# A one-core mLSTM and two MLPs: first MLP in five passes, 512 columns a product in three, stacked scores, a new order

## Chip, core and metric

The kernel runs on one core of a Trainium2 chip. The metric is device time in microseconds (us) of one execution; the profiled execution has a span inside it, from the first to the last instruction.

## What is computed

Three stages follow each other. `S`=768, `H`=8 heads, `D`=40, two batches; 1536 tokens reach the MLPs.

```python
def _attn_ref(q, k, v, i_gate, f_gate, o_gate):          # per batch and head, step t:
    m_new = maximum(f[t] + m, i[t])
    C = exp(f[t] + m - m_new) * C + exp(i[t] - m_new) * outer(v[t], k[t])
    n = exp(f[t] + m - m_new) * n + exp(i[t] - m_new) * k[t]
    y[t] = sigmoid(o_gate[t]) * (C @ q[t]) / maximum(abs(n @ q[t]), 1.0)

x = y as (1536, 320)
x = ((x @ w_a) * (x @ w_b)) @ w_out                      # first MLP, 1536 hidden
h = x @ w_in;  out = (h * sigmoid(h)) @ w_out2           # second MLP, 2048 hidden
```

## The kernel before

**Units.** The tokens are cut into twelve units of 128 (`u` = chunk * 2 + batch; chunk `c` of six). The recurrence is done by chunk: scores of a unit (`scores`, part `uN.s0`/`.s1`, four heads each), weighed with the decays (`weigh`), summed with the values (`values`), plus what the state of the chunk before gives (`carried`); `update` makes the part that the state gains. The result is transposed (`x_product`, `uN.px`) and split into a high and a low part (`.xh`, `.xl`) in `xring`, 128 columns a unit.

**Decays.** `uN.d0`/`.d1` is a scan on DVE. For units 0 and 1 its input is made in PSUM by TensorE (`factors`, tile `fb_u`); for the ten others it is a 512 KB broadcast read of `fsd` from DRAM into the SBUF tile `e_u`, and the scan reads and writes that tile.

**Precision.** MLP operands are split in two fp32r halves, so that an MLP product is a group of such matmuls: a first-layer product (`first_layer`, tile `h`) is eight matmuls with different weights, a second-layer product (`second_layer`, tile `acc`) three for each unit. Scores, values and states are plain fp32 matmuls, which the trace records as two records each.

**Weights.** Each of the twelve hidden blocks `j` of the first MLP comes as two 64-bit loads (`lwJ.a`, `.b`), is narrowed by ACT and DVE, and its low halves are subtracted by POOL (`rest`: `w_j` 128x512 and 128x320, `tl_j` 64x128 twice).

**Passes.** A pass `mP` takes a block of units through a range of `j`: products `a` and `b` on TensorE, eviction `e` (ACT), gate `g` (DVE), high half `h` (ACT), low half `l` (POOL), second layer `c`. There are eleven: three blocks of two units (256 columns) over `j` 0 to 4, again over 5 to 7, again over 8 to 11, then two blocks of three units (384 columns) over all `j`. The second MLP (`n0` to `n2`) has three blocks of four units (512 columns).

**Order.** Every part is issued by a list written out in the file (`ORDER`); each engine, and SP's DMA queue, runs its share of it in that order. Thirty of the parts (`f0` to `f29`) are fills: four bf16 matmuls on TensorE (tile `warm`) whose result nobody reads.

Of the kernel before, what the change touches and what calls it, by code (L numbers as in the profile page):

```python
# [8 lines left out]
F32 = mybir.dt.float32  # L9
# [7 lines left out]
PASSES = ((0, range(0, 5)),  # L17
          (1, range(0, 5)),
          (2, range(0, 5)),
          (0, range(5, 8)),  # L20
          (1, range(5, 8)),
          (2, range(5, 8)),
          (0, range(8, 12)),
          (1, range(8, 12)),
          (2, range(8, 12)),
          (3, range(0, 12)),
          (4, range(0, 12)))


# [3 lines left out]
lf zeros const li run0 run1 expi0 f26 f3 f8 expf0 f1 pg0 lw0.b l0.t f10 f2 f6 lw0.a w0.ap w0.bp w0.bs w0.bo w0.as  # L33
u1.f0 u0.f1 u0.f0 u0.d0 w0.t1 expf1 w0.hb l0.q l1.k l0.k u0.s0 l1.q f27 f25 l1.t u1.s0 u1.s1 lw2.b lw1.b w0.ao
starts u0.sv sel f13 w0.u1 lw2.a w0.t0 w0.u0 l2.q lw1.a w0.v0 w0.v1 w0.ha w0.la u0.d1 u1.sv u0.sk w0.lb u1.d0 f22
f16 u1.f1 u1.d1 u1.sk f28 f17 u0.s1 f15 f7 f23 f29 f21 expi1 u0.w1 f4 u0.si f12 u0.sig u1.si u0.v1 w1.bp w2.bs w1.bs
w1.bo u1.sig w2.bp u1.az w1.t1 w1.u1 w1.t0 w1.u0 w1.hb w1.lb u0.w0 u0.v0 w2.as w2.bo w2.hb f20 u0.cb f9 w2.t0 w2.u0
w2.t1 w2.ap u1.w1 u1.v1 u1.w0 prod u0.da u0.dn u1.v0 u1.cb u1.upd u1.ai1 u1.ai2 f24 u0.upd u1.ai0 u0.ai0 u1.da
u0.ai2 w2.ao u0.om w2.u1 u0.rc u0.ox u0.xt u0.ai1 w2.ha u1.dn u1.rc u1.om u1.ox w2.lb u1.xt lw5.a lw3.b pg1 u3.si
u2.ao0 l2.e u2.d0 w1.as w1.ap w1.ao u0.px u0.xh l2.k f5 f11 f18 u2.s1 u2.s0 f0 u1.px u2.si u2.car f14 u1.xh w1.ha  # L40
u2.ao1 l2.t u2.sk u2.sv u2.upd u2.w1 u2.v1 w3.bs w2.v0 l4.q lw3.a u0.az u2.ai1 u1.xl l3.e w1.v0 u0.xl w2.la m0.2.a
w3.bp w3.as u2.ai0 u2.w0 u2.v0 u2.cb w2.v1 m0.2.b w1.la u2.az w3.bo w3.hb w3.t1 w3.u1 w3.lb u3.az u3.d0 l3.k l3.q
u3.car u3.s1 u2.sig u2.cc m0.2.e m0.2.g w3.t0 u2.ai2 u2.om w3.ap w3.ao u3.cb u2.da u2.dn u2.rc m0.0.a u2.ao2 m0.0.b
m0.0.e m0.0.g w3.u0 l3.t u3.sk u3.s0 u3.w0 w1.v1 m0.1.b lw4.b w4.bs w4.bp m0.2.h w4.bo m0.1.a u3.sv u3.v0 m0.2.l
# [85 lines left out]
def tile_mlstm_gated_mlps(ctx: ExitStack, tc: tile.TileContext, i_gate, f_gate, q_cols, k_cols, kvo, w1, w2,  # L130
                          out):
    nc = tc.nc
# [9 lines left out]
    GR = G * D  # L142
    GH = (0, 3, 5)
    SLOT = {h: (h // G, h % G) if h < 6 else (2, h - 5) for h in range(H)}
    BLOCKS = {1: (2, 2, 2, 3, 3), 2: (4, 4, 4)}
    UNITS, AT = {}, {}
    for m, sizes in BLOCKS.items():
        for blk, n in enumerate(sizes):
# [708 lines left out]
```

## Time and profile before

| | |
|---|---|
| median of three runs | 471.05 us (465.54, 471.05, 472.09) |
| profiled execution | 465.23 us, its span 463.5 us |
| TensorE (PE) busy | 454.5 us, 98% of the span |
| weight loads (PEld) | 435.9 us, 94% |
| POOL, ACT, DVE | 239.2, 219.1, 160.7 us |

Busy is the union of an engine's instructions, so that overlapped matmuls aren't counted twice. The mean of one matmul is longer than the distance from one to the next, since they are pipelined: what a matmul costs in a dense stretch is read from starts, not from its own length.

### The profile page before, as it was taken

The page shows a single profiled execution, that of the slowest core. Times are in us where ns is not written, and L with a number is a line of the kernel's source. Part 1 is how long each engine was busy: PE and PEld are TensorE (multiplying, and loading weights), DVE is VectorE, ACT ScalarE, POOL GpSimd, SP SyncE. Part 2 cuts the span into 40 slices and gives each one's busy share as a digit, 9 for nine tenths or more (in the row PEclk, how much of TensorE's full clock was granted, in tenths as well). Part 3 has the DMA queues.
Part 4 walks back from the last instruction along what each step waited for, and adds up shares of the span by engine and source line. Part 5 has one row for each costly group of instructions (what it writes and reads, how often), then busy time and mean ns, then how long its engine had stood idle before and what let it go on. Part 6 is the DMA issues. An engine that isn't in the chain of part 4 may idle for free.

```text
span 463.5 us, 7966 instructions
## 1 busy us (share of the span) xinstructions
PE 454.5 (98%) x3103; PEld 435.9 (94%) x3103; DVE 160.7 (35%) x268; ACT 219.1 (47%) x507; POOL 239.2 (52%) x278
## 2 busy tenths in 40 slices
PE   7999999999999999999999999999999999999996
PEld 6999999999999999999999999999998989998996
DVE  7876665252435465335442342314300000000000
ACT  4867777756421230232553565656634332443333
POOL 5667795666643465152443557468733343332433
PEclk9989999999999999999999999999999999999999
DMA  7887928351003241231233132133001000010001
GB/s 241 286 243 209 311 88 263 106 177 54 1 9 114 51 141 43 85 106 64 93 102 117 64 100 89 63 126 124 2 0 58 0 2 0 1 42 1 0 16 57
DMA packets 25089, 42.30 MB, mean 91 GB/s; under 512 B 2156, under 2 KB 18348, under 8 KB 25052
## 3 DMA queue, kind: packets, MB, share of 16 engines
q1 hardware_dynamic: 25052, 41.80, 28.4%
q8 instruction: 24, 0.39, 0.4%
q14 instruction: 13, 0.11, 0.1%
HBM read 38.99 MB, written 2.02 MB: 88 GB/s over the span
## 4 chain that ended last, share of the span: by engine, by line
PE 88%; DMA 7%; ACT 1%; DVE 1%; issue 1%; SPq 1%; POOL 0%; POOLq 0%; ACTq 0%
PE h L643 46%; PE acc L654 10%; PE acc L652 10%; PE acc L653 10%; PE y_u L491 4%; PE s_u L478 3%; DMA raw_j<-in_w_dram 3%; DMA e_u<-fsd 2%; PE px_u L614 1%; PE ups_u L511 1%; DMA w_j<-tl_j 1%; PE y_u L501 1%; DMA qT_u<-in_q_cols_dram 1%; DVE e_u L453 0%; SPq L230 0%
## 5 line engine op out<-in xcount | busy, mean ns | idle before, releaser
L643 PE MATMUL h<-xring,w_j 128*128 128x256 f32 (+2 forms) x1088 | 179.3, 317 | 0.1
L643 PEld LDWEIGHTS h<-xring,w_j 128*128 128x128 f32 x1088 | 161.9, 190 | 5.0 <-DMA w_j<-tl_j 0.3
L281 POOL TENSOR_TENSOR g2w<-gw,g2w 128x512 fp32r<-128x512 f32 x48 | 63.2, 1323 | 85.7 <-ACT g2w L688 83.7
L281 POOL TENSOR_TENSOR g<-g,g 128x256 fp32r<-128x256 f32 (+1 forms) x60 | 56.0, 941 | 66.6 <-ACT g L688 65.2
L281 POOL TENSOR_TENSOR w_j<-cvt_j,w_j 128x320 fp32r<-128x320 f32 (+3 forms) x72 | 62.6, 877 | 30.7 <-ACT w_j L342 13.1
L643 PE MATMUL h<-xeven,w_j 128*128 128x512 f32 x256 | 62.6, 392 | 0.0
L654 PE MATMUL acc<-w_j,g2w 128*128 128x320 f32 x192 | 59.4, 309 | 0.1
L652 PE MATMUL acc<-w_j,g2w 128*128 128x320 f32 x192 | 59.4, 310 | 0.0
L653 PE MATMUL acc<-w_j,g2w 128*128 128x320 f32 x192 | 59.3, 309 | 0.0
L688 ACT CAST g<-g 128x256 fp32r<-128x256 f32 (+1 forms) x60 | 26.6, 448 | 68.0 <-DVE g L682 46.1
L643 PEld LDWEIGHTS h<-xeven,w_j 128*128 128x128 f32 x256 | 47.1, 188 | 8.8
L684 ACT ACTIVATE gw<-h 128x512 f32<-128x512 f32 x48 | 28.5, 596 | 55.2 <-PE h L643 45.1
L682 DVE TENSOR_TENSOR g<-a,h 128x256 f32<-128x256 f32 (+1 forms) x60 | 28.2, 472 | 75.6 <-PE h L643 45.7
L652 PE MATMUL acc<-w_j,g 128*128 128x320 f32 x144 | 45.5, 316 | 0.0
L688 ACT CAST g2w<-gw 128x512 fp32r<-128x512 f32 x48 | 29.8, 621 | 32.4 <-PE acc L654 31.9
L654 PE MATMUL acc<-w_j,g 128*128 128x320 f32 x144 | 44.7, 310 | 0.3 <-POOL g L281 0.3
L653 PE MATMUL acc<-w_j,g 128*128 128x320 f32 x144 | 44.4, 308 | 0.0
L653 PEld LDWEIGHTS acc<-w_j,g2w 128*128 128x128 f32 x192 | 36.0, 188 | 1.0
L652 PEld LDWEIGHTS acc<-w_j,g2w 128*128 128x128 f32 x192 | 36.1, 188 | 1.0
L674 ACT ACTIVATE a<-h 128x256 f32<-128x256 f32 (+1 forms) x60 | 24.9, 423 | 25.6 <-PE h L643 24.8
L654 PEld LDWEIGHTS acc<-w_j,g2w 128*128 128x128 f32 x192 | 36.0, 188 | 0.4 <-POOL g2w L281 0.4
L281 DVE TENSOR_TENSOR xeven<-px_u,xeven 128x384 fp32r<-128x384 f32 x8 | 4.5, 557 | 68.5 <-ACT xeven L621 68.5
(100 smaller groups left out, 595.9 us busy)
## 6 DMA issues: line engine op xcount, KB each, us to landing
raw_j<-in_w_dram SPq DMA_DIRECT2D x16, 704.0 KB
raw_j<-in_w_dram SPq DMA_DIRECT2D x12, 512.0 KB
kvo_u<-in_kvo_dram SPq DMA_DIRECT2D x12, 480.0 KB
raw_j<-in_w_dram SPq DMA_DIRECT2D x12, 448.0 KB
e_u<-fsd SPq DMA_DIRECT2D x10, 512.0 KB
qT_u<-in_q_cols_dram SPq DMA_DIRECT2D x12, 180.0 KB
kz<-in_k_cols_dram SPq DMA_DIRECT2D x36, 60.0 KB
out_dram<-osb SPq DMA_DIRECT2D x12, 160.0 KB
```

The source lines that it names most:

```text
L281: return eng.tensor_tensor(out=out_, in0=x, in1=hi.bitcast(F32), op=ALU.subtract)
L478: nc.tensor.matmul(out=s[:, i], lhsT=kz[u % 2][:, j, g], rhs=un["q", u][:, g], start=True, stop=True)
L491: nc.tensor.matmul(out=T["y1"][:, h], lhsT=un["e", u][:, h], rhs=T["v"][:, h], start=True, stop=True)
L501: nc.tensor.matmul(out=y2[:, GH[g] + lo:GH[g] + G], lhsT=un["q", u][:, g], rhs=cb[:, g, lo:G], start=True, stop=True)
L643: nc.tensor.matmul(out=po, lhsT=w[:, wi * P:(wi + 1) * P], rhs=xt[:, :, xi], start=(n == 0), stop=(n == len(pairs) - 1))
L652: nc.tensor.matmul(out=o, lhsT=hi, rhs=w[:, off:off + DM], start=first, stop=False)
L653: nc.tensor.matmul(out=o, lhsT=hi, rhs=w[:, off + DM:off + 2 * DM], start=False, stop=False)
L654: nc.tensor.matmul(out=o, lhsT=lo, rhs=w[:, off:off + DM], start=False, stop=last)
L674: nc.scalar.activation(out=A[j], in_=A.pop(("p", j)), func=ACT.Copy, scale=WS ** -2)
L682: nc.vector.tensor_tensor(out=Q[j], in0=A.pop(j), in1=PB.pop(j), op=ALU.mult)
L684: nc.scalar.activation(out=Q[j], in_=PB.pop(j), func=ACT.Silu, scale=1 / WS)
L688: nc.scalar.copy(out=G2[j][:, 0], in_=Q[j])
```

## The change

Five passes instead of eleven: units 0 and 1 over `j` 0 to 4, units 2 and 3 over 0 to 4, units 0 to 3 over 5 to 11, then 4 to 7 and 8 to 11 over all `j`. The last three have 512 columns a product. `xring` grows from six to eight units and takes the second MLP's even blocks too (tile `xeven` is gone). From unit 6 on q and k are loaded stacked: 120 rows that hold the 40 dimensions in three parts, of which one is made the low half, so that one fp32r matmul gives the score of a head. Units 2 and 3 get their decay factors from TensorE too (`FB` = 2). The state update is one masked product on DVE and POOL for all units; ACT's part of it is gone. A part may name its engine in the list (`:v` DVE, `:p` POOL). `ORDER` is another list throughout.

```diff
-PASSES = ((0, range(0, 5)),
-          (1, range(0, 5)),
-          (2, range(0, 5)),
...
-          (3, range(0, 12)),
-          (4, range(0, 12)))
...
+PASSES = (((0, 2), range(0, 5)),
+          ((2, 4), range(0, 5)),
+          ((0, 4), range(5, 12)),
+          ((4, 8), range(0, 12)),
+          ((8, 12), range(0, 12)))
...
-    RING = 6
+    RING = 8
...
+    kz = [keys(F32, f"kz{i}") for i in range(2)]
+    STACK = ((0, 0, D), (D, 0, KT - D), (KT, 0, D), (KT + D, KT - D, D))
+
+    def load_stack(u, x):
+        b, c, s = place(u)
+        t = raws.tile([P, G * G * C], F32, tag="raw", name=f"st{x}_u{u}")[0:GR]
+        un["st", u, x] = t.rearrange("p (j g t) -> p j g t", j=G, g=G)
+        src = (q_cols, k_cols)[x][b, c].rearrange("(j d) g t -> d j (g t)", j=G)
+        for row, lo, hi in STACK:
+            nc.sync.dma_start(out=t[row:row + hi - lo].rearrange("p (j x) -> p j x", j=G), in_=src[lo:hi])
...
+    def copy(out_, in_):
+        e = how.get("e", "a")
+        if e == "a":
+            nc.scalar.copy(out=out_, in_=in_)
+        else:
+            (nc.vector if e == "v" else nc.gpsimd).tensor_copy(out=out_, in_=in_)
+
+    def both(out_, x, y, op):
+        (nc.vector if how.get("e") == "v" else nc.gpsimd).tensor_tensor(out=out_, in0=x, in1=y, op=op)
...
         def factors(n):
-            if c > 0:
+            if c >= FB:
                 return
...
+        def stack_high(x):
+            T["sh", x] = keys(F32R, f"sh{x}_u{u}")
+            copy(T["sh", x], un["st", u, x])
+
+        def stack_low(x):
+            r = slice(x * KT, x * KT + D)
+            rest(T["sh", x][r], un["st", u, x][r], T["sh", x][r])
+
         def scores(n):
             s = bank(f"s_u{u}", P, 4, C)
+            T["s", n] = s
+            if u >= PLAIN:
+                for i in range(4):
+                    g, j = SLOT[4 * n + i]
+                    nc.tensor.matmul(out=s[:, i], lhsT=T["sh", 1][:, j, g], rhs=T["sh", 0][:, j, g],
+                                     start=True, stop=True)
+                return
...
-            if u < BUSY:
-                d.update(az=adv_zero, **{f"ai{j}": lambda j=j: adv_in(j) for j in range(G)})
-            else:
-                d.update(am=adv_mask)
+            d.update(am=adv_mask)
```

**What the new list does to the engines.** First TensorE, where it takes up unit 6 (its scores are the `s_u` rows on line 478 before and 487 after; `h` is the first layer, `acc` the second). Before:

```order
L643 MATMUL h<-xring,w_j_1048 128x256 x8
L478 MATMUL s_u_1846<-qT_u_1124,kz_102 128x128 x4
L643 MATMUL h<-xring,w_j_1258 128x256 x8
L652 MATMUL acc<-w_j_1046,g_1843 128x320
L653 MATMUL acc<-w_j_1046,g_1843 128x320
L654 MATMUL acc<-w_j_1046,g_1843 128x320
```

After:

```order
L638 MATMUL h<-xring,w_j_955 128x512 x8
L487 MATMUL s_u_1282<-sh_u_1105,sh_u_942 128x128 x4
L647 MATMUL acc<-w_j_533,g_1239 128x320
L648 MATMUL acc<-w_j_533,g_1239 128x320
L649 MATMUL acc<-w_j_533,g_1239 128x320
```

The first layer stands here with 512 columns instead of 256, and the scores take both operands from the stacked tiles `sh_u`.

TensorE again, where the gate columns (`pg`, `pgb`) have just been made. Before:

```order
L407 MATMUL pg<-ident,scratch 128x16
L416 MATMUL pgb<-scratch 120x6 x6
L614 MATMUL px_u_480<-ident,x_u_432 128x128 x3
L425 LDWEIGHTS idb
L425 MATMUL warm<-idb 128x128
```

After:

```order
L445 MATMUL fb_u_463<-scratch,ident 128x128 x4
L408 MATMUL pg<-ident,scratch 128x16 x10
L417 MATMUL pgb<-scratch 120x6 x6
L445 MATMUL fb_u_498<-scratch,ident 128x128 x4
L612 MATMUL px_u_512<-ident,x_u_444 128x128 x3
L492 MATMUL s_u_517<-qT_u_346,kz_98 128x128 x4
```

Two of the four new calls of `factors` (for units 3 and 2) stand around them now, and the scores of unit 2 follow without a fill between.

Last POOL, where it takes up units 2 and 3 (`kvo_u` with `e_u` is the scaling of k, with `y_u` the output gate; `vx_u` the scaling of v; `cn` the state; `w_j` and `tl_j` low halves of weights). Before:

```order
L471 TENSOR_TENSOR kvo_u_531<-kvo_u_531,e_u_472 128x320
L465 TENSOR_TENSOR vx_u_518<-kvo_u_531,isg 128x8x40
L520 MEMSET cn_u_423 120x41
L281 TENSOR_TENSOR w_j_373<-cvt_j_0_389,w_j_373 128x512
L281 TENSOR_TENSOR w_j_357<-cvt_j_0_477,w_j_357 128x512
L520 MEMSET cn_u_553 120x41
L281 TENSOR_TENSOR tl_j_598<-cvt_j_1_570,w_j_595 64x128
```

After:

```order
L279 TENSOR_TENSOR cn_b_419<-cn_b_419,gb 120x369
L279 TENSOR_TENSOR vx_u_490<-kvo_u_460,isg 128x8x40
L279 TENSOR_TENSOR kvo_u_460<-kvo_u_460,e_u_331 128x320
L276 CAST w_j_308<-cvt_j_0_468 128x512
L279 TENSOR_TENSOR vx_u_525<-kvo_u_523,isg 128x8x40
L279 TENSOR_TENSOR w_j_308<-cvt_j_0_468,w_j_308 128x512
```

POOL has gained the scaling of the old state (120x369) and a 128x512 high half that ACT made before; the small memsets are gone.

## Rows read from the trace of the kernel before

**Rows 1.** The page's busy us, share of the span and instructions of each engine.

```profile
PE 454.5 (98%) x3103; PEld 435.9 (94%) x3103; DVE 160.7 (35%) x268; ACT 219.1 (47%) x507; POOL 239.2 (52%) x278
```

**Rows 2.** Windows: length, busy us of PE, PEld, DVE, ACT, POOL, clock, DMA share, GB/s.

```profile
0.00:20.00 20.00, 16.35 (x161) 15.95 (x161) 15.49 (x26) 12.02 (x25) 11.25 (x28) 1.00 0.80 255
20.00:40.00 20.00, 19.32 (x175) 18.82 (x175) 16.04 (x28) 14.08 (x42) 13.68 (x20) 0.91 0.82 245
40.00:60.00 20.00, 19.59 (x157) 18.93 (x156) 13.22 (x20) 14.57 (x41) 15.44 (x17) 1.00 0.88 281
60.00:80.00 20.00, 19.31 (x164) 19.09 (x164) 10.90 (x25) 14.62 (x40) 14.83 (x22) 1.00 0.51 150
80.00:100.00 20.00, 20.00 (x160) 19.98 (x160) 7.30 (x13) 13.90 (x37) 12.77 (x16) 1.00 0.57 184
```

**Rows 3.** Timeline of PE, dense products: start, length, line, tiles, shape, count.

```profile
86.15 4.96 PE L643 MATMUL h<-xring,w_j 128*128 128x256 f32 x40
90.95 0.31 PE L652 MATMUL acc<-w_j,g 128*128 128x320 f32 x1
...
92.71 2.08 PE L643 MATMUL h<-xring,w_j 128*128 128x256 f32 x16
...
229.91 4.35 PE L643 MATMUL h<-xring,w_j 128*128 128x384 f32 x24
234.10 0.31 PE L652 MATMUL acc<-w_j,g 128*128 128x320 f32 x1
...
385.72 3.81 PE L643 MATMUL h<-xring,w_j 128*128 128x512 f32 x16
389.37 0.30 PE L652 MATMUL acc<-w_j,g2w 128*128 128x320 f32 x1
```

**Rows 4.** Timeline of PE, small products and fills, each with its successor.

```profile
14.42 1.11 PE L444 MATMUL fb_u<-scratch,ident 128*128 128x128 f32 x8
15.36 0.61 PE L425 MATMUL warm<-idb 128*128 128x128 bf16 x8
...
16.76 1.73 PE L425 MATMUL warm<-idb 128*128 128x128 bf16 x28
18.32 1.04 PE L491 MATMUL y_u<-vx_u,e_u 128*128 128x41 f32 x8
...
59.84 1.05 PE L478 MATMUL s_u<-qT_u,kz 120*128 120x128 f32 x8
60.65 2.16 PE L643 MATMUL h<-xring,w_j 128*128 128x256 f32 x16
...
66.34 0.98 PE L491 MATMUL y_u<-vx_u,e_u 128*128 128x41 f32 x8
67.14 0.88 PE L501 MATMUL y_u<-cn_u,qT_u 120*128 120x123 f32 x6
```

**Rows 5.** Timeline of PE, its wait ahead of unit 3's `carried`.

```profile
37.53 0.87 PE L501 MATMUL y_u<-cn_u,qT_u 120*128 120x123 f32 x6 [0.68 <-DVE e_u L453]
```

**Rows 6.** Timeline of POOL, 0 to 75 us.

```profile
8.60 0.72 POOL L465 TENSOR_TENSOR vx_u<-kvo_u,isg 128x320 f32<-128x320 f32 x1 [0.97 <-DVE isg L409]
...
42.08 1.44 POOL L281 TENSOR_TENSOR g<-g,g 128x256 fp32r<-128x256 f32 x2 [0.85 <-ACT g L688]
43.87 0.98 POOL L281 TENSOR_TENSOR tl_j<-cvt_j,w_j 64x128 fp32r<-64x128 f32 x2 [0.35 <-ACT w_j L304]
...
47.83 0.98 POOL L545 TENSOR_TENSOR cn_u<-cn_u,cd_u 120x369 f32<-120x369 f32 x1
49.79 1.28 POOL L281 TENSOR_TENSOR w_j<-cvt_j,w_j 128x512 fp32r<-128x512 f32 x1 [0.98 <-ACT w_j L293]
53.38 2.98 POOL L281 TENSOR_TENSOR tl_j<-cvt_j,w_j 64x128 fp32r<-64x128 f32 x2
...
62.67 0.86 POOL L281 TENSOR_TENSOR w_j<-cvt_j,w_j 128x320 fp32r<-128x320 f32 x1
```

**Rows 7.** Timeline of DVE at the same time: a scan that reads SBUF alone.

```profile
53.81 2.29 DVE L453 TENSOR_TENSOR_SCAN e_u<-e_u,ident 128x1024 f32<-128x1024 f32 x1 [0.91 <-DMA e_u<-fsd]
```

More of the change, by code (lines that the diff above doesn't have):

```diff
@@ L144, in tile_mlstm_gated_mlps @@
     SLOT = {h: (h // G, h % G) if h < 6 else (2, h - 5) for h in range(H)}
[L145 to L148, printed above, removed]
-            lo = sum(sizes[:blk])
-            UNITS[m, blk] = range(lo, lo + n)
-            AT.update({(m, u): (blk, u - lo) for u in range(lo, lo + n)})
-    NB1, NB2 = len(BLOCKS[1]), len(BLOCKS[2])
+    LAST = PASSES[-1][0][0]
+    NB2 = NT // 4
     J1, J2 = w1.shape[0], w2.shape[0]
@@ L187, in tile_mlstm_gated_mlps @@
     fsd = dram.tile([BH, S], F32, name="fsd")
-    x1 = {u: const.tile([P, 3 * P], F32, name=f"x1_{u}") for u in range(NT) if AT[1, u][0] < NB1 - 1}
+    x1 = {u: const.tile([P, 3 * P], F32, name=f"x1_{u}") for u in range(LAST)}
     def place(u):
@@ L303, in tail_hi @@
             p, q_, s_ = where(n)
-            nc.scalar.copy(out=tile_()[p, s_], in_=B["c"][p, 0:P])
+            copy(tile_()[p, s_], B["c"][p, 0:P])
         def tail_lo(n):
@@ L562, in gate_out @@
         def gate_out():
-            nc.gpsimd.tensor_tensor(out=un["o", u], in0=un["o", u], in1=T["y"][:, :, 0:D], op=ALU.mult)
+            both(un["o", u], un["o", u], T["y"][:, :, 0:D], ALU.mult)
         def magnitudes():
@@ L583, in chunk @@
                  px=lambda: x_product(1, u, T["x"]), xh=lambda: x_high(1, u), xl=lambda: x_low(1, u), d0=lambda: decays(0))
-        if c == 0:
+        if u >= PLAIN:
+            d.update({f"h{'qk'[x]}": lambda x=x: stack_high(x) for x in range(2)})
+            d.update({f"l{'qk'[x]}": lambda x=x: stack_low(x) for x in range(2)})
+        if c < FB:
             d.update(f0=lambda: factors(0), f1=lambda: factors(1), d1=lambda: decays(1))
-        else:
+        if c > 0:
             d.update(car=carried, cc=combine_add)
@@ L770, in tile_mlstm_gated_mlps @@
         parts.update({f"u{u}.{n}": f for n, f in ch[u].items()})
-        for n, f in (("q", load_q), ("k", load_k), ("t", load_kvo)):
+        for n, f in (("q", load_q), ("t", load_kvo)):
             parts[f"l{u}.{n}"] = lambda f=f, u=u: f(u)
-        if u >= B:
+        if u < PLAIN:
+            parts[f"l{u}.k"] = lambda u=u: load_k(u)
+        else:
+            parts.update({f"l{u}.s{'qk'[x]}": lambda u=u, x=x: load_stack(u, x) for x in range(2)})
+        if u >= FB * B:
             parts[f"l{u}.e"] = lambda u=u: load_fs(u)
@@ L794, in tile_mlstm_gated_mlps @@
         for t in ORDER:
+            t, _, e = t.partition(":")
+            how.clear()
+            if e:
+                how["e"] = e
             parts[t]()
```

327 lines of the change are left out of this document (149 added, 178 removed).

## The prediction

> **What bounds the kernel now.** I read the busy times first [rows 1]: PE 98% of the span, no other engine above 52%. The windows of the first 100 us [rows 2] say where the missing 2% are: PE is idle for 5.4 of these 100 us (20 x 5 less the 94.6 that the five rows add up to), and in the second row the granted clock is 0.91, which is 3.6 of 20 us at 1.2 in place of 2.4 GHz, some 1.8 us of work lost. In the last of these rows PE is never idle, and of the 9 us that it idles in the span [rows 1] only 3.6 are left for everything behind it, the last output included. So time is PE's work plus some 7 us at the start. A change gains what it takes off PE's work, and loses what makes PE wait; the other engines count only as far as they do that. The third thing to see is how hard they run: in a 20 us window DVE reaches 80% (16.0), POOL 77% (15.4) and ACT 74% (14.8) at most [rows 2].
>
> I work in the profiled execution, 465.2 us. The runs beside it are 465.5, 471.1 and 472.1, so the median stands 1.3% above it.
>
> **First layer in wide products.** Column for column the work is the same; what changes is the number of matmuls. The price of one, from start to start [rows 3]: 256 columns (90.95 - 86.15) / 40 = 0.120 us, 384 columns (234.10 - 229.91) / 24 = 0.1746, 512 columns (389.37 - 385.72) / 16 = 0.228. Each lies 13 to 15 ns above its columns at 2.4 GHz, a fixed part that wide products pay less often. Before: 36 pass-blocks of 16 matmuls with 256 columns and 24 with 384, 576 x 0.120 + 384 x 0.1746 = 136.2 us. After: 10 with 256 and 31 with 512, 160 x 0.120 + 496 x 0.228 = 132.3. The second layer has as many matmuls as before. **Term: -3.9.** The Trainium skill (TensorE: Matmul & The Clock Gate, Back-to-back issue gap) gives a fixed part of about 2.5 ns for a warm matmul; by it the 304 matmuls saved would bring 0.8 us, and the sum would be 3.1 higher. The rows stand against it.
>
> **Stacked scores.** Six units of eight heads. Now a head costs two records, (60.65 - 59.84) / 4 = 0.2025 us [rows 4]. fp32r with 128 columns isn't in the trace. From below: a bf16 matmul of that shape, (18.32 - 16.76) / 28 = 0.056 [rows 4]. From above: no gain at all, 0.2025; nothing makes one fp32r matmul dearer than two fp32 records. I take the row that is nearest in what it must load: a record of `values` has 41 columns to stream and still costs (67.14 - 66.34) / 8 = 0.100 [rows 4], so that loading 128 columns of four-byte weights sets it, and the stacked score has the same weights to load, once. 48 x (0.2025 - 0.100) = 4.9. **Term: -4.9**, between 0 and -7.0.
>
> What this needs elsewhere: twelve copies of 120x1152 on ACT, twelve subtractions on POOL (in the next part but one), 48 loads in place of 18, 4.5 MB more in all. Loads go through SP in order and take one of the four `raw` buffers, so weights behind them come later; DMA engines are used to 51 and 57% in the two last windows [rows 2], so I cost the bytes at nothing. Without that cover weights 9 to 11 would come late, which would add to the POOL term below. The stacked tiles share two buffers with `kz`: unit 7's copy waits on ACT for the last score of unit 6, and the casts of `g` behind it wait as well; PE has the wide products of the pass over units 0 to 3 meanwhile. The same goes for `xring`: the second MLP's first columns wait for the last product of the pass over units 4 to 7, with five `j` of the last pass in front of their first reader. Both at nothing.
>
> **Factors of units 2 and 3.** Sixteen more fp32 matmuls, 32 records at (15.36 - 14.42) / 8 = 0.1175 [rows 4]: +3.8 on PE. They remove two broadcast reads and the 0.7 us for which PE waited behind unit 3's scan [rows 5]. If they all lay where fills lay before, the term would be -0.7; I take the dearer end, since fills move to later places and stay 30 in number. **Term: +3.8**, down to -0.7.
>
> **The new order: POOL.** This is the step I trust least. Take the place where the wide pass over units 0 to 3 sums its product for `j` = 5, the second of its second-layer groups. Ahead of it PE has 313 small records at 0.100, 64 of `factors` at 0.1175, 120 fill matmuls at 0.056, 160 of 256 columns at 0.120, 56 of 512 at 0.228 [rows 3, 4] and 72 of 320 columns at (92.71 - 90.95) / 12 = 0.147 [rows 3]: 31.3 + 7.5 + 6.7 + 19.2 + 12.8 + 10.6 = 88 us. With the losses of before (5.4 + 1.8) PE would be there at 95.3.
>
> POOL must by then have done, counted in its new order and priced where it runs undisturbed [rows 6]: 22 `tl` at 0.49, 11 of 320 columns at 0.86, 10 of 512 (one a cast) and two `g` of 512 at 1.28, ten `g` of 256 at 0.72, 21 on `kvo`/`vx` at 0.72, eight on `cn` at 0.98, three stacked subtractions at 2.7 (the step from 320 to 512 columns, 2.2 ns a column, carried on to 1152), 15 small ones at 0.3: 10.8 + 9.5 + 15.4 + 7.2 + 15.1 + 7.8 + 8.1 + 4.5 = 78 us. Its first product of use starts at 8.6 [rows 6]. 78 of 86.7 us is 90%; before, it ran at 71% from 20 to 100 us (56.7 of 80) [rows 2]. At 80%, the best that any engine but PE shows, it is there at 8.6 + 97.5 = 106.1, 11 us late, and PE, which needs the low half for its third matmul, stands with it. A longer queue should run fuller than POOL did, since it then waits less for work: I take half way between 80 and 90%, 85%, 100.4. **Term: +5**, between 0 and +15.
>
> POOL can also be held by DVE: two `tl` took 2.98 us while a scan with two SBUF inputs ran, and 0.98 without [rows 6, 7]. The Trainium skill (SBUF — State Buffer, SBUF: two separate sides) has this as a rule: DVE and POOL share a port pair that one instruction locks for its whole length, a DVE instruction with two SBUF inputs among them. The trace agrees, with these 2 us. The change makes the scans of units 2 and 3 read PSUM, which speaks for it; units 4 to 7 keep theirs ahead of the place above. I leave both within the 85%.
>
> ACT loses the state update (30 small products) and gains the stacked copies; DVE gains six masked products. Neither reaches PE's load ahead of that place, so both cost nothing as long as POOL is the later one.
>
> **Sum.** 465.2 - 3.9 - 4.9 + 3.8 + 5 = 465.2: no change in the profiled execution. Since two of three runs of before stood at 471 to 472, I put the forecast between the two levels, at 467. A measurement of this kernel can tell some 2% from no change, 9.3 us.
>
> **Rivals.**
> *POOL doesn't fill up.* It stays at the 77% of its best window: 8.6 + 78 / 0.77 = 109.9, 14.6 late. 465.2 - 5.0 + 14.6 = 474.8; at the 71% of the whole stretch 118.5, 23 late, 483. The forecast turns into slower when PE loses 14.3 us, which is POOL below 77%. For it: no engine beside PE went above 80% in a window. Against it: much of POOL's idle time before was for lack of work, and the list is free to place its parts anywhere. Chance 0.20.
> *POOL hides, the start gets shorter.* No POOL term, the factors lie in fill time: 465.2 - 3.9 - 4.9 - 0.7 = 455.7, at the 2% line; with scores at the bf16 price 453.6. For it: 6.7 us of fills show slack at the start. Against it: 12 of 30 fills now stand after the first product of the MLP, where PE had no slack. Chance 0.22, a bit over half of it beyond the line.
> *The stacked scores save nothing.* 128 columns in fp32r take as long as two fp32 records: 465.2 + 4.9 = 470.1, POOL's extra work for nothing. Against it: the records of `values`. Chance 0.10, within 2%.
> *The forecast*, PE's gain eaten by waits for POOL between 50 and 110 us: 0.48, within 2%.
>
> That makes faster 0.13, same 0.67, slower 0.20. The range runs from 455 (the second rival) to 480 (the first rival at 77%, 474.8, in a run at the upper level, 1.2% on top); about 0.1 is left out on either side.
>
> **What the profile of the changed kernel would show.** First layer: 496 matmuls of 512 columns, 0.228 from start to start. Scores: four `s_u` records of unit 6 within 0.4 us; 0.8 would make the third rival right. Waits: PE's idle time for POOL (`g`, `w_j`) between 40 and 110 us, together 3 to 8 us, POOL above 80% in these windows; none at all is the second rival, 15 us the first. After 130 us PE should again be without idle time; if waits stand there, on `xring` or on the stacked tiles, the two edits that I cost at nothing were wrong. A clock of 0.5 in the 40 to 100 us stretch would make every wait dearer than I counted.

## The result, and the profile after

The changed kernel takes 471.4 us in the median of 20 executions, the kernel before 465.4 in as many: a ratio of 1.0124, 95% interval 1.0099 to 1.0148. It is 1.2% slower, where I forecast no change of the profiled execution. The time lies in the range. The profiled execution has 469.27 us and a span of 467.5, 4.0 more than before.

Busy times and the hardware queue (packets, MB, share) of the page after; [rows 1] are those of before, whose queue moved 41.80 MB:

```profile
PE 453.1 (97%) x2783; PEld 412.9 (88%) x2783; DVE 175.0 (37%) x278; ACT 197.8 (42%) x399; POOL 276.7 (59%) x294
...
q1 hardware_dynamic: 26968, 46.29, 33.6%
```

Windows of after, in the columns of [rows 2]:

```profile
0.00:20.00 20.00, 15.04 (x136) 14.30 (x137) 14.91 (x25) 13.27 (x25) 12.16 (x32) 1.00 0.81 246
20.00:40.00 20.00, 19.27 (x153) 18.81 (x153) 17.09 (x27) 11.52 (x27) 14.48 (x23) 0.83 0.71 221
40.00:60.00 20.00, 19.53 (x174) 19.19 (x173) 13.95 (x29) 12.62 (x34) 16.73 (x23) 1.00 0.81 238
60.00:80.00 20.00, 16.83 (x132) 16.49 (x131) 9.72 (x16) 9.67 (x24) 13.62 (x16) 0.91 0.41 112
80.00:100.00 20.00, 20.00 (x145) 18.38 (x145) 12.49 (x20) 11.45 (x25) 16.30 (x15) 1.00 0.99 245
```

And every wait of PE in after, from its timeline (idle before the row, and what ended it, in brackets):

```profile
2.54 3.60 PE L426 MATMUL warm<-idb 128*128 128x128 bf16 x32 [2.54 <-DVE idb L725]
6.42 1.20 PE L445 MATMUL fb_u<-scratch,ident 128*128 128x128 f32 x8 [0.28 <-ACT scratch L385]
11.23 2.22 PE L492 MATMUL s_u<-qT_u,kz 120*128 120x128 f32 x16 [2.13 <-DMA kz<-in_k_cols_dram]
28.91 0.79 PE L408 MATMUL pg<-ident,scratch 16*128 16x16 f32 x10 [0.73 <-DVE cn_b L535]
54.15 3.12 PE L638 MATMUL h<-xring,w_j 128*128 128x256 f32 x24 [0.47 <-DVE g L679]
64.05 3.25 PE L492 MATMUL s_u<-qT_u,kz 120*128 120x128 f32 x16 [3.17 <-DMA qT_u<-in_q_cols_dram]
106.83 0.41 PE L649 MATMUL acc<-w_j,g 128*128 128x320 f32 x1 [1.59 <-POOL g L279]
```

Span and mean granted clock, first of before, then of after:

```profile
core 0: 463.5 us, clock 0.996
core 0: 467.5 us, clock 0.989
```

Three sums tell where the 4 us are. PE's idle time rose from 9.0 to 14.4 us (span less busy; 3.4 us of it lie behind the last product in both). The span times the mean granted clock, which counts a stretch at 1.2 GHz at what it would take at 2.4, is 463.5 x 0.996 = 461.6 before and 467.5 x 0.989 = 462.4 after: the lower level costs 1.9 us before, 5.1 after. So PE's work at the full level is 461.6 - 9.0 = 452.6 before and 462.4 - 14.4 = 448.0 after. **The work fell by 4.6 us (5.0 forecast), and 5.4 us more of standing still and 3.2 us more of the lower clock ate it.** Over all executions the mean clock is 0.986 in after, and 0.993 to 0.996 in those of before that ran beside the experiments, so the clock's part is no accident of one profile.

The long wait, in the chain of waits (start, length, what): unit 5's q goes out at 57.08 and needs 6.84 us.

```profile
51.42 5.64 DMA raw_j<-in_w_dram
57.08 6.84 DMA qT_u<-in_q_cols_dram
64.05 3.25 PE s_u L492 x16
```

What SP had issued ahead of it, in its timeline: two weight halves, and four loads of unit 6's stacked k, which the kernel before did not have (the rows left out are small copies of weight parts).

```profile
51.42 0.38 SPq L219 DMA_DIRECT2D raw_j<-in_w_dram  x1
...
52.45 0.54 SPq L219 DMA_DIRECT2D raw_j<-in_w_dram  x1
53.22 1.51 SPq L193 DMA_DIRECT2D st_u<-in_k_cols_dram  x4
...
57.08 0.34 SPq L177 DMA_DIRECT2D qT_u<-in_q_cols_dram  x1
```

The four loads cost q twice. SP spends 1.5 us on issuing them; then, by its list of waits, it stands 0.6 us at the small copy behind them until a load of k v o has landed, and 1.3 us at q until the weight load of 51.42 has. In both waits that is the transfer eight places ahead in SP's order, and four of the eight are the stacked loads.

Sixteen score products behind the wait take 3.25 us; at the full clock, in the chain at 40.66, eight take 0.89. And the wait at 106.83, one second-layer group ahead of the place that my POOL term named (the group of `j` = 7, which the list sets before that of 5), hangs on POOL, but POOL had been idle for a load:

```profile
97.77 0.73 POOL L279 TENSOR_TENSOR vx_u<-kvo_u,isg 128x320 f32<-128x320 f32 x1
102.92 0.74 POOL L279 TENSOR_TENSOR kvo_u<-kvo_u,e_u 128x320 f32<-128x320 f32 x1 [4.42 <-DMA kvo_u<-in_kvo_dram]
```

### The profile page after: what moved, and what is told of

Read it like the earlier page. It is cut to its first block, busy times and chain, and to the rows that moved or that the text cites. A ratio compares the mean times of both kernels' runs of the same rounds, so it can differ in the third digit from the quotient of the medians.

```text
span 467.5 us, 7268 instructions
## 1 busy us (share of the span) xinstructions
PE 453.1 (97%) x2783; PEld 412.9 (88%) x2783; DVE 175.0 (37%) x278; ACT 197.8 (42%) x399; POOL 276.7 (59%) x294
## 4 chain that ended last, share of the span: by engine, by line
PE 84%; DMA 9%; POOL 3%; SPq 1%; DVE 1%; issue 1%; ACT 0%; POOLq 0%; ACTq 0%
PE h L638 43%; PE acc L649 10%; PE acc L647 10%; PE acc L648 10%; DMA kvo_u<-in_kvo_dram 4%; PE y_u L504 3%; DMA qT_u<-in_q_cols_dram 2%; PE s_u L492 2%; PE px_u L612 1%; DMA e_u<-fsd 1%; DMA raw_j<-in_w_dram 1%; PE y_u L514 1%; PE ups_u L524 1%; PE s_u L487 1%; POOL w_j L279 1%
## 5 line engine op out<-in xcount | busy, mean ns | idle before, releaser
L638 PE MATMUL h<-xring,w_j 128*128 128x512 f32 (+1 forms) x1040 | 237.3, 377 | 0.5 <-DVE g L679 0.5
L638 PEld LDWEIGHTS h<-xring,w_j 128*128 128x128 f32 x1040 | 181.6, 188 | 31.2 <-DVE g L679 0.6
L279 POOL TENSOR_TENSOR g<-g,g 128x512 fp32r<-128x512 f32 (+1 forms) x41 | 52.3, 1279 | 21.7 <-ACT g L274 20.7
L274 ACT CAST w_j<-cvt_j 128x320 fp32r<-128x320 f32 (+3 forms) x75 | 31.9, 447 | 34.7 <-DVE cvt_j L245 18.1
L679 DVE TENSOR_TENSOR g<-g,h 128x512 f32<-128x512 f32 (+1 forms) x41 | 25.4, 620 | 51.8 <-PE h L638 41.0
L622 DVE TENSOR_TENSOR xring<-px_u,xring 128x384 fp32r<-128x384 f32 x24 | 13.0, 554 | 72.4 <-ACT xring L274 68.9
L279 POOL TENSOR_TENSOR sh_u<-st_u,sh_u 40x1152 fp32r<-40x1152 f32 x12 | 32.1, 2676 | 4.1 <-issue 3.3
L274 ACT CAST g<-g 128x512 fp32r<-128x512 f32 (+1 forms) x30 | 16.4, 547 | 32.6 <-DVE g L679 20.7
L649 PEld LDWEIGHTS acc<-w_j,g 128*128 128x128 f32 x144 | 27.1, 188 | 1.8 <-POOL g L279 1.8
## 6 DMA issues: line engine op xcount, KB each, us to landing
raw_j<-in_w_dram SPq DMA_DIRECT2D x12, 448.0 KB
```

The source lines that it names most:

```text
L274: nc.scalar.copy(out=out_, in_=in_)
L279: (nc.vector if how.get("e") == "v" else nc.gpsimd).tensor_tensor(out=out_, in0=x, in1=y, op=op)
L622: nc.vector.tensor_tensor(out=xt[:, 3:6], in0=px.pop(u), in1=xt[:, 0:3].bitcast(F32), op=ALU.subtract)
L638: nc.tensor.matmul(out=po, lhsT=w[:, wi * P:(wi + 1) * P], rhs=xt[:, :, xi], start=(n == 0), stop=(n == len(pairs) - 1))
L649: nc.tensor.matmul(out=o, lhsT=lo, rhs=w[:, off:off + DM], start=False, stop=last)
L679: nc.vector.tensor_tensor(out=Q[j], in0=Q[j], in1=PB.pop(j), op=ALU.mult)
```

## The experiments

Theory L: the loads of the stacked tiles, costed at nothing, come ahead of others in SP's order and on the DMA engines, and PE pays with waits and with the clock behind them. The expectations call its main part, unit 5's late q, theory Q. Rival P: POOL's work bounds PE up to 107 us. A second theory, S, for the rest: the start of the new order stands still for unit 0's k.

All runs side by side. The ratio goes by 20 executions of after and by 4 to 12 of each other kernel; the interval is the 95% one. The times in the middle are PE's waits in the profiled execution alone, and the clock is the mean granted in it. That execution need not be a typical one: that of q5_early took 470.94 us where the median is 467.3, that of q5_s3 465.27 where it is 468.51.

| run | ratio to before | wait at the start | for unit 5's q | at 90 to 115 us | clock |
|---|---|---|---|---|---|
| after | 1.0124 (1.0099 to 1.0148) | 2.13 | 3.17 | 1.59 | 0.989 |
| q5_early | 1.0034 (0.9999 to 1.0070) | 3.60 | 0 | 1.18, 2.12 | 0.985 |
| sk6_behind | 1.0052 (1.0015 to 1.0089) | 5.22 | 0 | 1.53 | 0.989 |
| plain_scores | 1.0072 (1.0033 to 1.0110) | 2.91 | 0 | 0 | 0.993 |
| plain8 | 1.0002 (0.9972 to 1.0032) | 4.08 | 0 | 0 | 0.989 |
| fb1 | 1.0179 (1.0126 to 1.0232) | 3.97 | 4.03 | 1.01 | 0.971 |
| narrow | 1.0242 (1.0216 to 1.0268) | 3.44 | 3.39 | 0.62 | 0.986 |
| pool_more | 1.0163 (1.0131 to 1.0195) | 2.30 | 3.25 | 0.38, 2.22 | 0.989 |
| q5_lv | 1.0063 (1.0028 to 1.0099) | 3.46 | 0 | 2.62 | 0.989 |
| q5_t6 | 1.0048 (1.0005 to 1.0091) | 2.31 | 0 | 3.08 | 0.991 |
| start_k | 1.0230 (1.0198 to 1.0261) | 3.59 | 4.39 | 0.82 | 0.982 |
| start_q5 | 1.0173 (1.0144 to 1.0202) | 5.70 | 0 | 0.95 | 0.978 |
| q5_s2 | 1.0043 (1.0005 to 1.0081) | 1.40, 2.01 | 0 | 0.77, 2.04 | 0.985 |
| q5_s3 | 1.0050 (1.0014 to 1.0087) | 2.76 | 0 | 1.34 | 0.996 |
| q5_fills | 1.0122 (1.0074 to 1.0170) | 3.65 | 0 | 1.40 | 0.993 |
| q5_warm | 1.0009 (0.9966 to 1.0053) | 1.60 | 0 | 1.45 | 0.996 |
| q5_t6_warm | 1.0028 (0.9997 to 1.0059) | 2.03 | 0 | 1.42, 0.98 | 0.996 |
| plain8_warm | **0.9936 (0.9901 to 0.9971)** | 1.48 | 0 | 0 | 0.996 |
| plain8_warm2 | 0.9967 (0.9939 to 0.9994) | 1.29 | 0 | 0 | 0.996 |

Unit 4's q is the one that is a little late in plain_scores, plain8, q5_fills, q5_warm and q5_t6_warm (0.31, 0.32, 0.86, 0.16, 0.30 us).

**Unit 5's q.** `q5_early`:

```diff
-w3.v0 l4.k l4.q u4.s0 ... lw7.a l6.sk w5.v1 l5.q u5.s0
+w3.v0 l4.k l4.q l5.q u4.s0 ... lw7.a l6.sk w5.v1 u5.s0
```

> One change to the kernel after: unit 5's q load is issued right behind unit 4's, ahead of the load of the eighth weight's second half and of the four stacked loads of unit 6. Theory Q (the loss is the late q of unit 5: TensorE waits 3.17 us for it at 64.05, and then 16 score products take 3.25 us at the lower clock): the wait and the fall of the clock behind it go, about 5 us, and the ratio to the kernel before comes from 1.012 to 1.002 (0.998 to 1.006). Rival P (GpSimd is the bound up to 107 us, and the 3.17 us are only where its lateness was spent): TensorE arrives 3 us earlier at the second-layer group at 107 and waits there 4 to 5 us in place of 1.6, the ratio stays at 1.010 to 1.013.

1.0034: the wait for q is gone, as theory L has it. The wait at 107 is 2.12 in place of 1.59, and 3.3 with a new one of 1.18 us for DVE ahead of it. That comes near rival P's 4 to 5 us, but the ratio does not come near P's 1.010: its interval ends at 1.0070.

`sk6_behind` leaves q where it is and moves only the four stacked loads.

```diff
-lw7.a l6.sk w5.v1 l5.q u5.s0
+lw7.a w5.v1 l5.q l6.sk u5.s0
```

> One change to the kernel after: the four stacked loads of unit 6 are issued behind unit 5's q in place of ahead of it. Theory Q with the stacked loads as the cause: unit 5's q comes 3 us earlier or more, its wait falls from 3.17 us to under 0.7 us, the ratio to 1.002 to 1.006. If the queue is held by the weight tile's transfer ahead of it and not by these four loads, the wait stays over 2 us and the ratio at 1.010 to 1.014.

1.0052, no wait for q. In this execution the start was 3.1 us later and q still went out at 56.95.

```profile
55.84 0.54 SPq L219 DMA_DIRECT2D raw_j<-in_w_dram  x1
...
56.95 0.58 SPq L177 DMA_DIRECT2D qT_u<-in_q_cols_dram  x1
```

q goes out 1.1 us behind the second weight half here, 4.6 in after, and 7.2 us before PE is ready for it (64.11), 3.8 in after (60.88). So the four loads ahead were enough to make it late.

**The stacked scores, whole and in part.** `plain_scores` and `plain8` (the l.k and l.q of the units come back, their stacked parts go):

```diff
-    PLAIN = 6
+    PLAIN = 12   # plain_scores; 8 in plain8
```

> One change to the kernel after: units 6 to 11 compute their scores as units 0 to 5 do, in fp32, and the stacked loads, copies and subtractions are gone, so TensorE has 48 x (0.2025 - 0.100) = 4.9 us more of score products and GpSimd and VectorE some 12 copies and 12 subtractions less. Theory Q: the 4.9 us come back, but unit 5's q is no longer behind four stacked loads, so its wait and the clock's fall, 5 us, go: ratio 1.008 to 1.016. If the stacking saved nothing: 1.000 to 1.004. If the wait stays although the four loads are gone: 1.020 to 1.025.

> One change to the kernel after: units 6 and 7 compute their scores as units 0 to 5 do, units 8 to 11 stacked as in after. Of the stacked scores' 4.9 us a third, 1.6 us, is given up; the stacked tiles of units 6 and 7, 2 x 16 loads and four subtractions of 2.7 us ahead of 110 us, are gone. If these loads are what makes unit 5's q and unit 6's k v o late, both waits (3.17 and 1.59 us) and the clock's fall at the first go: ratio 0.999 to 1.004, 3.3 us under the run with all scores plain (1.0072). If not: 1.010 or more.

Both go theory L's way: 1.0072, just better than its range, and 1.0002 with only units 6 and 7 plain, within it. In both PE has no wait of more than 0.4 us from 35 us on; these are all waits of `plain8`:

```profile
2.54 3.47 PE L426 MATMUL warm<-idb 128*128 128x128 bf16 x32 [2.54 <-DVE idb L725]
6.41 1.13 PE L445 MATMUL fb_u<-scratch,ident 128*128 128x128 f32 x8 [0.40 <-ACT scratch L385]
13.09 3.75 PE L492 MATMUL s_u<-qT_u,kz 120*128 120x128 f32 x16 [4.08 <-DMA kz<-in_k_cols_dram]
33.45 0.79 PE L408 MATMUL pg<-ident,scratch 16*128 16x16 f32 x10 [0.72 <-DVE cn_b L535]
55.37 1.13 PE L492 MATMUL s_u<-qT_u,kz 120*128 120x128 f32 x8 [0.32 <-DMA qT_u<-in_q_cols_dram]
```

`plain8` takes copies and subtractions away too, so the next runs ask POOL alone.

**POOL's work.** `pool_more`, and `q5_lv` (on q5_early):

```diff
-w3.ha u1.ox u1.xt:p w3.la f0
+w3.ha u1.ox u1.xt:p w3.la w3.la f0      # also w4, w5, w6, w7, w9
```
```diff
-u6.hk u6.lk ... u6.lq ... u7.hk u7.lk ... u7.hq u7.lq
+u6.hk u6.lk:v ... u6.lq:v ... u7.hk u7.lk:v ... u7.hq u7.lq:v
```

> One change to the kernel after: six of the weights' low subtractions on GpSimd are issued twice, with the same result, 7.7 us more of GpSimd work ahead of 107 us. If GpSimd bounds TensorE up to there, as my sum's term of 5 us had it, all of it comes on top: ratio 1.025 or more. If GpSimd has slack up to 60 us and is late only at the group at 107 (1.59 us): 1 to 4 us more, ratio 1.014 to 1.021.

> The kernel with unit 5's q early, and the four stacked subtractions of units 6 and 7, some 2.7 us each on GpSimd, made by VectorE. GpSimd has 11 us less to do ahead of 107 us. Theory P (what is left of the predicted term is GpSimd's lateness at the group at 107, 2.1 us there): that wait goes, ratio 0.997 to 1.001 against 1.0034. Rival: VectorE, which has 1.18 us of lateness at 97 us already, gets later by as much, ratio 1.002 to 1.006.

7.7 us more of POOL's work cost 0.4% (1.0163 against 1.0124), 1.8 us, and the intervals overlap; all 7.7 would be 1.7%. Four subtractions fewer gained nothing (1.0063 against 1.0034), though DVE got their work. In `q5_lv` two of the four subtractions, 5.4 us, lie ahead of 107 (not all 11 us of the expectation), and POOL stands for unit 6's k v o all the same:

```profile
101.06 0.74 POOL L279 TENSOR_TENSOR kvo_u<-kvo_u,e_u 128x320 f32<-128x320 f32 x1 [4.58 <-DMA kvo_u<-in_kvo_dram]
```

Rival P falls: POOL's queue has slack, and at 107 us it is late because a load is.

**Unit 6's k v o.** `q5_t6`, on q5_early:

```diff
-l7.q l7.t w9.la ... l6.e l7.sq l6.t u6.d0
+l7.q l7.t l6.t w9.la ... l6.e l7.sq u6.d0
```

> The kernel with unit 5's q early, and unit 6's k v o load issued right behind unit 7's, ahead of the stacked loads of unit 7. In the trace after GpSimd sat 4.42 us until 102.92 for that load, which took 8.19 us from 94.57, and TensorE's wait of 1.59 us at 106.83 hung on it. If so, the wait at 107 (2.12 us with unit 5's q early) goes: ratio 0.998 to 1.001. If GpSimd is simply full there: no change, 1.002 to 1.005.

1.0048, no gain. The wait at 107 went, but DVE, in its timeline, then waited for unit 7's decay read, and PE 3.08 us for the `xring` write behind it. The DMA engines are full there (0.99 from 80 to 100 us in after, 0.57 in [rows 2]): what is moved ahead makes the next load late.

```profile
93.06 2.29 DVE L454 TENSOR_TENSOR_SCAN e_u<-e_u,ident 128x1024 f32<-128x1024 f32 x1 [6.65 <-DMA e_u<-fsd]
95.26 0.53 DVE L622 TENSOR_TENSOR xring<-px_u,xring 128x384 fp32r<-128x384 f32 x1
```

**The other two terms.** `narrow` cuts the 512-column products of the first layer in two, `fb1` loads the factors of units 2 and 3 again (`l2.e` and `l3.e` come back in the list, the four `factors` parts go):

```diff
-            nc.tensor.matmul(out=po, lhsT=w[:, wi * P:(wi + 1) * P], rhs=xt[:, :, xi],
...
+        step = 2 if w.shape[1] == WN else 4
+        for lo in range(0, nt // P, step):
...
+                nc.tensor.matmul(out=po[:, lo:lo + step], lhsT=w[:, wi * P:(wi + 1) * P], rhs=xt[:, lo:lo + step, xi],
```
```diff
-    FB = 2
+    FB = 1
```

> One change to the kernel after: the 496 first-layer products of 512 columns are cut into 992 of 256 again. By the pitches read from the kernel before, 0.120 us for 256 columns and 0.228 for 512, TensorE gets 496 x (2 x 0.120 - 0.228) = 6.0 us more: ratio 1.023 to 1.027. If wide products save nothing: 1.010 to 1.014.

> One change to the kernel after: the decay factors of units 2 and 3 are loaded by broadcast from the chip's memory again and not made by 32 matmuls of TensorE. 32 x 0.128 us = 4 us of TensorE work go. If nothing else waits: ratio 1.003 to 1.006. The loads come at 25 to 40 us, where the DMA engines are busy at 0.8 to 1.0 of the time in the trace after, so units 2 and 3 may wait for them: up to 5 us, ratio up to 1.016.

`narrow` costs 0.0118 x 465.4 = 5.5 us. `fb1` missed its first range: 4 us less of PE's work, and yet no faster than after (the intervals overlap), with a wait of 4.03 us for q and a clock of 0.72 from 20 to 40 us. Two broadcast reads more, in a stretch whose DMA engines are busy at 0.71 in after and at 0.84 in `fb1`, cost at least what 32 matmuls do.

**The start.** `start_k` loads unit 0's k and q first; `start_q5` has q5_early's edit besides.

```diff
-f10 l1.t expi0 pg0 ... l0.q l0.t ... l0.k u0.s1
+f10 l0.k l0.q l1.t expi0 pg0 ... l0.t ... u0.s1
```

> One change to the kernel after: unit 0's k and q are loaded first of all tiles, ahead of unit 1's k v o and of the first weight. In the profiled executions of the new order so far TensorE waits for unit 0's k at 9 to 14 us: 2.13, 3.60, 5.22, 2.91 and 3.97 us, and in the worse ones the clock falls behind it; the kernel before has no such wait. Theory S (this wait, other in every execution, is the second part of the loss): it goes or falls under 1 us, the span shortens by 2 to 5 us and the scatter of the times with it: ratio to before 1.002 to 1.008 in place of 1.012. Rival: the next operand of unit 0 (its v and decay factors) is late by as much, the ratio stays at 1.010 or above.

> Both edits on the kernel after: unit 0's k and q first, and unit 5's q right behind unit 4's. If the late start (2 to 5 us) and unit 5's q with the clock's fall (4.2 us in the first of these experiments, 1.0124 to 1.0034) are separate, they add up: ratio 0.992 to 0.998, the first version under the time of before. If GpSimd bounds the first 107 us, the gain at the start is lost again at the second-layer group there, where the wait grows from 2.1 us to 4 or more, and the ratio stays at 1.002 to 1.005.

Both missed badly. SP now stops at the k load until the k tile has been cleared, and every load behind it goes out late: the first k v o at 5.17 us, where it went out at 1.71 in after. SP's timeline in `start_k`:

```profile
1.26 0.40 SPq L749 DMA_DIRECT2D scratch<-in_f_gate_dram  x1
3.72 1.03 SPq L199 DMA_DIRECT2D kz<-in_k_cols_dram  x3
4.80 0.33 SPq L177 DMA_DIRECT2D qT_u<-in_q_cols_dram  x1
5.17 0.40 SPq L204 DMA_DIRECT2D kvo_u<-in_kvo_dram  x1
```

`q5_s2` and `q5_s3` (on q5_early) move these loads without that stop, half and all the way ahead of the first weight.

```diff
-lw0.b ... lw0.a w0.as w0.ap w0.t0 w0.u0 l0.q l0.t u0.sv u0.sig ... l0.k u0.s1       # q5_s2
+lw0.b ... l0.q l0.t u0.sv u0.sig l0.k lw0.a w0.as w0.ap w0.t0 w0.u0 ... u0.s1
```
```diff
-l1.t expi0 pg0 u1.sv u1.sig lw0.b w0.bs w0.bp w0.bo ... lw0.a ... l0.q l0.t u0.sv u0.sig ... u0.d0 u0.f1 u0.d1 l0.k u0.s1       # q5_s3
+l1.t l0.q l0.t expi0 pg0 u1.sv u1.sig l0.k lw0.b w0.bs w0.bp u0.d0 u0.f1 u0.d1 u0.sv u0.sig w0.bo ... lw0.a ... u0.s1
```

> The kernel with unit 5's q early, and one more move: unit 0's q, k v o and k are issued between the two halves of the first weight, not behind both, so 448 KB less stand ahead of them (1.2 us at the 370 GB/s of 10 to 15 us in the trace after) and the queue does not stop for the clearing of the k tile, as it did when k came first of all (3.72 us in place of 1.7). Theory S (the start is the second part of the loss): TensorE's wait for unit 0's k, 2.1 to 5.2 us so far, falls by 1 us or more, ratio 0.998 to 1.002 against 1.0034. Rival: the wait for the first weight's second half on ScalarE and GpSimd takes its place, ratio 1.003 or more.

> The kernel with unit 5's q early, and unit 0's q, k v o and k ahead of both halves of the first weight, behind unit 1's k v o; VectorE's and GpSimd's steps for unit 0 stand ahead of those for that weight. Some 900 KB less ahead of k, 2.4 us at 370 GB/s, less 0.6 us in which the queue waits for the clearing of the k tile. Theory S: the wait for unit 0's k is under 1 us, nothing else of the start is late, the clock's fall behind it is gone: 2 to 5 us, ratio 0.993 to 0.999. Rival: the first weight, 3 us later, holds ScalarE and VectorE in their order, and TensorE waits for unit 0's scores and values: ratio 1.003 or more.

1.0043 and 1.0050, both as the rivals had it. (The 370 GB/s of both expectations are those of 4 to 6 us in after, 367; from 10 to 15 us the trace has 275.) In `q5_s3` k is in time, and PE waits 2.76 us at 15.61 for unit 0's scaled k instead. The loads can't all come first, so `q5_warm` leaves them and puts ten fill parts into the wait.

```diff
-l0.k u0.s1
+l0.k f0 f1 f2 f3 f4 f5 f6 f7 f8 f9 u0.s1
```

> The kernel with unit 5's q early, and 40 more fill products ahead of unit 0's first scores, where TensorE sat 2.1 to 5.2 us with nothing to do; 40 x 0.056 = 2.2 us, so they cost nothing to 0.1 us. If the clock falls behind that wait because TensorE had stood still, it stays up at 12 to 18 us, the mean granted clock rises by 0.003 to 0.006, 1.5 to 3 us: ratio 0.996 to 1.000. If the fall has another cause: 1.002 to 1.005.

1.0009, just outside the 0.996 to 1.000 that were expected. The interval overlaps that of q5_early, but the mean clock of the 12 executions rises from 0.991 to 0.995, and the windows show where; first two rows of `q5_early`, 8 to 16 us, then of `q5_warm` (clock third from the end):

```profile
8.00:12.00 4.00, 1.02 (x8) 0.83 (x8) 3.49 (x5) 2.81 (x7) 1.59 (x4) 1.00 1.05 285
12.00:16.00 4.00, 3.38 (x15) 3.27 (x16) 1.42 (x3) 3.30 (x7) 3.80 (x9) 0.57 0.98 265
```
```profile
8.00:12.00 4.00, 3.25 (x48) 3.06 (x48) 3.47 (x5) 2.75 (x7) 1.46 (x3) 1.00 1.04 273
12.00:16.00 4.00, 3.15 (x31) 3.13 (x32) 2.09 (x5) 3.49 (x7) 3.77 (x8) 1.00 1.04 272
```

`q5_fills` tried fills between the gate columns' small products: 1.0122, 4 us dearer than q5_early, more than the fills' own 1.5, and the clock still falls (0.92 from 20 to 40 us; mean of its runs 0.990, of q5_early's 0.991).

```diff
+            if not first:
+                warm(3)                     # ahead of each pair of pg
...
+                warm(1)                     # ahead of each pgb
```

> The kernel with unit 5's q early, and 27 fill products of 128 columns set between the small products of the gate columns, behind which the granted clock falls to 0.5 for 6 to 7 us in every profile so far, before's too (from 30.7 us in after, from 22.7 in before). The fills cost 27 x 0.056 = 1.5 us of TensorE. If they keep the clock at full level the 3.4 us of the fall are saved: ratio 0.998 to 1.001. If the fall comes all the same: 1.005 to 1.008.

`q5_t6_warm` (both edits) gave 1.0028; the gains did not add up.

> Unit 5's q early, unit 6's k v o early and 40 fills in the wait at the start together. If the gains add up: ratio 0.991 to 0.997, the first version under the time of before. If the start's fall of the clock is not from standing still: 0.998 to 1.001.

**Both causes at once.** `plain8_warm` is `plain8` with q5_warm's edit.

> Units 6 and 7 with plain scores and 40 more fills ahead of unit 0's first scores. With the clock up at 12 to 18 us, as in the run with unit 5's q early and these fills (0.0025 less of the ratio): 0.995 to 0.999. If the two were one and the same loss: 1.000 to 1.003.

0.9936, a median of 463.4 us against 471.4 of after: 1.9% under after by the ratios, and a little faster than before, clear of the interval. PE's waits in it, all of them:

```profile
2.54 3.38 PE L426 MATMUL warm<-idb 128*128 128x128 bf16 x32 [2.54 <-DVE idb L725]
6.42 1.13 PE L445 MATMUL fb_u<-scratch,ident 128*128 128x128 f32 x8 [0.49 <-ACT scratch L385]
12.73 2.22 PE L492 MATMUL s_u<-qT_u,kz 120*128 120x128 f32 x16 [1.48 <-DVE e_u L454]
30.27 0.79 PE L408 MATMUL pg<-ident,scratch 16*128 16x16 f32 x10 [0.71 <-DVE cn_b L535]
53.92 3.13 PE L638 MATMUL h<-xring,w_j 128*128 128x256 f32 x24 [0.47 <-DVE g L679]
```

`plain8_warm2` has 12 more fills ahead of the gate columns.

```diff
-w1.ap pg1 u2.si:p
+w1.ap f20 f21 f22 pg1 u2.si:p
```

> The same with 12 more fills right ahead of the gate columns' small products, where TensorE waits 0.7 us for VectorE; 12 x 0.056 = 0.67 us, so they cost nothing. If the fall of the clock at 30 to 36 us (2.7 to 3.4 us lost) comes from that pause, it goes: 0.988 to 0.993. If it comes from the small products themselves, it stays: as the run without these fills.

0.9967 with a median of 463.5 us: no gain, and the two kernels can't be told apart, so the gain over before is 0.3 to 0.6%. In the profiled execution the pause ahead of the gate columns is gone and the clock from 20 to 40 us stays at 0.91, so it can fall there without that pause. Five of the 12 executions have a mean clock of 0.999 or 1.000, one of 12 without these fills; whether they help is open.

## Why the prediction was wrong

*First layer, -3.9: right.* `narrow` gives 11 ns for each of 496 matmuls saved (5.5 us), against 12 by the pitches. The Trainium skill (TensorE: Matmul & The Clock Gate, Back-to-back issue gap) has 2.5 ns for an isolated warm matmul, which would make 1.2 us; the run decides against it for this stream.

*Stacked scores, -4.9: right as work.* A stacked head costs (100.39 - 100.00) / 4 = 0.0975 us in after, 0.100 forecast; TensorE's timeline:

```profile
100.00 0.56 PE L487 MATMUL s_u<-sh_u,sh_u 120*128 120x128 f32 x4
100.39 0.84 PE L514 MATMUL y_u<-cn_b,qT_u 120*128 120x123 f32 x6
```

*Factors, +3.8: not refuted.* Work as a whole came out at -4.6 against -5.0. What the reads they replace would cost I had left out, and `fb1` shows that it is no less.

*The step that failed* is "Loads go through SP in order [...] so I cost the bytes at nothing". It named the right queue and the wrong victims: not weights 9 to 11, but unit 5's q (3.17 us, and 1.8 us by the clock of 0.91 in 60 to 80) and unit 6's k v o. I read the DMA engines' share of before in the windows from 60 to 100 us, 51 and 57%, though the loads stand ahead of 60, where [rows 2] has 0.88; and what counts is the order in the queue: from 50 to 64 us of after the share is 0.86 to 1.11 in each 2 us. It is shown by three edits (1.0034, 1.0052, 1.0002), two of which move nothing but loads. That it is the stacked loads and not ACT's copies is shown for the wait at 64 (`sk6_behind`). The wait at 107 goes when unit 6's k v o is moved ahead of unit 7's stacked q (`q5_t6`), so it hangs on that load's place. In `plain8`, with no stacked load ahead, that load goes out at 88.61 in place of 94.57; that the stacked loads alone make this difference is argued, not shown. The two other items at nothing held: behind 107 us PE stands still for 0.15 us in all up to its last product.

*The POOL term, +5: one group off, a third of the size, wrong cause.* 1.59 us at 106.83; POOL ran at up to 84% in a window (16.73 of 20) as forecast, but at 68% from 60 to 80, where PE stood for q. The price of its work was right (77.2 us of it up to 107 us, 78 counted), but 7.7 us more cost about 1.8, and its wait there is for a load. That the total came out only 4 us over the forecast is partly luck: the 5 us that I gave to POOL were lost to loads and the clock. One sign of the shared port stands in after: `g` of 128x256, 0.72 us by [rows 6], took 2.38 us at 92.65 beside DVE's scan of 92.20, in agreement with the Trainium skill (SBUF — State Buffer, SBUF: two separate sides).

*The clock.* My last sentence, that a clock of 0.5 would make every wait dearer, is what happened, and no term held it: 3.2 us in the profiled execution. About half of it stands in the stretch that I named (0.91 against 1.00 from 60 to 80); the rest is from 20 to 40, 0.83 against 0.91.

*The start* I took over from before. The new list sets 32 fill matmuls ahead of the first factors and none where unit 0's k is awaited; before, fills and 24 factor records filled that time:

```profile
5.47 1.46 PE L425 MATMUL warm<-idb 128*128 128x128 bf16 x12
6.72 4.01 PE L444 MATMUL fb_u<-scratch,ident 128*128 128x128 f32 x24
10.56 1.06 PE L478 MATMUL s_u<-qT_u,kz 120*128 120x128 f32 x8
```

With `q5_warm` and `plain8_warm` filling it the clock stays up. How much of the 1.2% it holds differs by execution (2.1 to 5.2 us of wait) and isn't settled to better than that.

*Open:* the fall of the clock at 30 to 37 us, in before at 22 to 26. Neither edit aimed at it (`q5_fills`, `plain8_warm2`) removed it from its profiled execution. It need not come: in `start_k`, whose clock is low from 15 to 29 us, the gate columns' products start at 35.63 and the clock is 1.00 from 30 to 44, and some executions of before have a mean clock of 1.000.

## What to carry to other kernels

When a change adds loads, write down for each DMA queue what now stands ahead of the next operand that the bound engine needs, and price its arrival from a row with a full queue (here 180 KB took 6.84 us); a low DMA share in a wide window says nothing on that. Count the loads too and not only their bytes: the stacked tile came in four, and two transfers behind it stood until the one eight places ahead of each had landed. A faster form of a product belongs where its preparation is free: the stacked scores paid in units 8 to 11 (1.0002 against 1.0072) and cost more than they gave in units 6 and 7 (1.0124 against 1.0002). Where TensorE must wait for a transfer anyway, fills in that wait cost nothing that these runs show, and kept its clock up (mean 0.992 in `plain8`, 0.996 in `plain8_warm`).

## What I had not expected of the hardware

Behind TensorE's waits at the start the granted clock stayed at 1.00 after 2.13, 2.30 and 2.76 us of standing still and fell after 2.91, 3.44, 3.60 and 4.08, as it did at 64 us after 3.17 (0.50 from 66 to 68). In `q5_s2` it fell behind two shorter waits, 1.40 and 2.01 us, so one wait's length does not settle it. The same load took different times in kernels with the same start: the wait for unit 0's k was 2.13 to 5.22 us with an unchanged list up to there. And an early load can be the worse one: 2 us of SP standing at one that isn't ready yet (`start_k`) cost 1.1%.
